# The second MLP's first product: seven block products a pair of ff chunks in place of eight, for two thirds of the tokens

## The chip, the cores and the metric

One Trainium2 chip, one core. The time is the device time of one launch in microseconds (us), the median of three runs. A profile of one more execution was taken by the hardware profiler; its times are from the start of its span.

## The reference

```python
# attention: q, k, v of 4 batches, 8 heads, 576 positions, 64 numbers a head;
# heads 0-3 look at the last 32 positions, heads 4-7 at every 4th of the last 128
x = attention(q, k, v)                            # (2304, 512) after the reshape
h = x @ moe_w_in;  r = np.maximum(h, 0.0)         # w_in (512, 2048)
x = (s * (r * r) + b) @ moe_w_out                 # w_out (2048, 512)
h = x @ moe2_w_in; g = h * np.cos(h)
return g @ moe2_w_out                             # (2304, 512)
```

## The kernel before

All numbers are fp32. A product in fp32 is made as three matmuls on parts cut in two (hi and lo, in the matmul's own fp32r format): hi·hi, hi·lo, lo·hi. Everything is kept transposed: features on the 128 partitions, tokens along the row. d_model = 512 is four chunks of 128, d_ff = 2048 is 16 ff chunks of 128.

**First MLP.** The tokens go through in five tiles `t` of 384, 384, 512, 512 and 512. A tile has 16 steps, one an ff chunk: `mm_in` makes h (PSUM, a ring of four banks from `bank`), `relu2` makes g and its two parts, and `mm_out` two steps later (LAG) adds to the four y banks. `relu2` takes ScalarE twice (Relu, then Square into r) and VectorE twice: a cast r → g hi (L496) and a subtraction r − g hi → g lo (L497). The attention of the next tile runs between the steps, in pairs of units ("duos", lists `DUO`): scores, softmax (`a_softmax`, `a_norm` on VectorE), transposition on TensorE (`a_transpose`, L350), and the product with v. `at((step, phase), f)` puts a piece of work behind a point of a step (phases 0, 1, 2). `y_out` scales a finished tile's y, and `y_park` sends it to DRAM (`y1`).

**The second MLP's weights** come as 64-bit words, and are prepared in the background of the first MLP by `w2_load`, `w2_float` (ScalarE), `w2_join` (VectorE) and `w2_cut`, at the steps listed in `BG_STEPS`. The 16 chunks of w_in, cut hi and lo, go to DRAM as `cut_in`. The 16 of w_out go to `whole_out`, and `job_load`, `job_sums` and `job_split` make from them the blocks that seven block products need (`cut_out`).

**Second MLP.** Three pieces of 768 tokens (i = 0, 1, 2). For each of the 48 (piece, ff chunk) pairs n, `mm_h` (L533) makes h in 24 matmuls of 128x384: four d_model chunks, three part products, two halves of 384 tokens. Then ScalarE and VectorE make h·cos(h) in four 128x768 operations: `cos_n` (ScalarE, the whole periods as int32), `cos_r` (VectorE, the rest), `cos_s` (ScalarE, Sin), `cos_g` (VectorE, times h). The product with w_out is made by seven block products where a plain one needs eight (Strassen's scheme in Winograd's form): 84 `unit`s of 12 matmuls of 128x384 (L642), `flush` forms sums of g, `unit_cut` cuts an operand hi (ScalarE cast, L587) and lo (VectorE subtraction, L588), `unit_load` brings 512 KB of `cut_out`. `evacuate`, `keep` and `send` empty PSUM and write the output through tile `o`, of which there are two. Units stand between the `mm_h`; those that are left run at the end, 26 of them.

All loads of weights (`wi` a chunk of `cut_in`, `wo` a unit's block), of x (`x_load`, 384 KB from `y1`) and the output's writes are issued by SyncE (SP), one after the other in program order: one that must wait for its buffer holds those behind it. `wi` and `wo` have four buffers each.

## Time and profile before

| what | before |
|---|---|
| time, median of 3 runs | 880.43 us (880.28 to 880.72) |
| the profiled execution | 880.15 us, of which 878.4 us are the span |
| TensorE (PE) busy | 870.6 us, 99%, 5148 matmuls |
| VectorE (DVE) busy | 594.2 us, 68% |
| ScalarE (ACT) busy | 477.1 us, 54% |
| the 16 DMA engines | 173.07 MB, mean 197 GB/s |

The span runs from the first to the last recorded event; the profiled time is longer by 1.75 us. A share is that engine's busy time over the span; PE's leaves 7.8 us of the span without a matmul. The first MLP runs to about 494 us; there the second MLP's h begins, and its 48 chunks and 84 units fill the rest.

### The profile page before, as it was taken

To read this page: it belongs to the slowest core of one execution; us is meant where nothing else is said; L and a number is where in the kernel's file an instruction comes from. 1 tells how busy PE (TensorE), PEld (TensorE's weight loads), DVE (VectorE), ACT (ScalarE), POOL (GpSimd) and SP (SyncE) were. 2 spreads that over 40 slices of the span, in tenths; PEclk is the share of its full clock that TensorE was granted. 3 is DMA by queue.
4 is the path that set the end of the run, shared out by engine and by line. 5 is a ranking of instruction groups with operands and counts; after the bars stand their busy time and mean duration, and the time that the engine had idled before them with its cause. 6 is when DMAs were issued, how large, how long until landed. Compare 5 with 4: busy or idle time off the path is not lost.

```text
span 878.4 us, 13747 instructions
## 1 busy us (share of the span) xinstructions
PE 870.6 (99%) x5148; PEld 778.9 (89%) x5148; DVE 594.2 (68%) x996; ACT 477.1 (54%) x1001; POOL 3.5 (0%) x10
## 2 busy tenths in 40 slices
...
PEclk9999999999999999999999999999999999999999
...
GB/s 251 337 231 252 95 93 148 96 103 157 151 127 125 111 200 165 167 135 148 262 321 386 344 359 121 140 218 188 183 226 214 203 185 172 206 220 146 219 268 209
DMA packets 76177, 173.07 MB, mean 197 GB/s; under 512 B 7152, under 2 KB 35280, under 8 KB 76112
## 3 DMA queue, kind: packets, MB, share of 16 engines
...
q8 instruction: 41, 0.67, 0.3%
...
## 4 chain that ended last, share of the span: by engine, by line
PE 94%; DVE 3%; ACT 1%; SPq 1%; DMA 1%; issue 0%; POOLq 0%; DVEq 0%
PE h L533 23%; PE yy_M L642 20%; PE h L424 6%; PE h L425 6%; PE h L426 6%; PE y L439 6%; PE y L441 6%; PE y L440 6%; PE y L436 4%; PE h L418 4%; PE sc L299 3%; PE pv L375 2%; PE tp L350 2%; DVE wa L148 1%; DVE wa L145 1%; DMA first_qk<-qk_d 1%
## 5 line engine op out<-in xcount | busy, mean ns | idle before, releaser
L533 PE MATMUL h<-x,wi 128*128 128x384 f32 x1152 | 205.1, 335 | 0.0
L533 PEld LDWEIGHTS h<-x,wi 128*128 128x128 f32 x1152 | 200.4, 188 | 0.2
L642 PE MATMUL yy_M<-op,wo 128*128 128x384 f32 x1008 | 180.2, 335 | 0.0
L642 PEld LDWEIGHTS yy_M<-op,wo 128*128 128x128 f32 x1008 | 175.7, 188 | 0.0
L542 ACT ACTIVATE i<-h 128x768 int32<-128x768 f32 x48 | 39.0, 813 | 149.1 <-PE h L533 149.1
L546 DVE SCALAR_TENSOR_TENSOR n<-i,h 128x768 f32<-128x768 int32 x48 | 45.8, 954 | 98.9 <-ACT i L542 98.9
L424 PE MATMUL h<-xs,wh 128*128 128x512 f32 (+1 forms) x256 | 98.7, 386 | 0.0
L439 PE MATMUL y<-g,wh 128*128 128x512 f32 (+1 forms) x256 | 97.7, 382 | 0.0
L426 PE MATMUL h<-xs,wl 128*128 128x512 f32 (+1 forms) x256 | 96.4, 376 | 0.0
L425 PE MATMUL h<-xs,wh 128*128 128x512 f32 (+1 forms) x256 | 96.3, 376 | 0.0
L441 PE MATMUL y<-g,wl 128*128 128x512 f32 (+1 forms) x256 | 96.2, 376 | 0.0
L440 PE MATMUL y<-g,wh 128*128 128x512 f32 (+1 forms) x256 | 96.1, 375 | 0.0
L588 DVE TENSOR_TENSOR op<-G,op 128x768 fp32r<-128x768 f32 x80 | 76.3, 955 | 19.0 <-ACT op L587 18.8
L587 ACT CAST op<-G 128x768 fp32r<-128x768 f32 x80 | 66.5, 833 | 36.2 <-PE yy_M L642 36.2
L329 ACT ACTIVATE sm<-sm,nmax 96x80 f32<-96x80 f32 (+1 forms) x140 | 49.5, 355 | 49.5 <-DVE nmax L326 49.5
L488 ACT ACTIVATE r<-h 128x512 f32<-128x512 f32 (+1 forms) x80 | 43.9, 549 | 48.5 <-PE h L426 40.9
L496 DVE CAST g<-r 128x512 fp32r<-128x512 f32 (+1 forms) x64 | 26.1, 408 | 55.9 <-ACT r L494 50.2
L560 DVE TENSOR_TENSOR G<-n,h 128x768 f32<-128x768 f32 x48 | 45.5, 949 | 15.9 <-ACT n L552 15.9
L424 PEld LDWEIGHTS h<-xs,wh 128*128 128x128 f32 x256 | 48.1, 188 | 7.8
L426 PEld LDWEIGHTS h<-xs,wl 128*128 128x128 f32 x256 | 48.1, 188 | 7.6
L441 PEld LDWEIGHTS y<-g,wl 128*128 128x128 f32 x256 | 48.0, 188 | 7.6
L425 PEld LDWEIGHTS h<-xs,wh 128*128 128x128 f32 x256 | 48.1, 188 | 7.3
...
## 6 DMA issues: line engine op xcount, KB each, us to landing
wo<-cut_out SPq DMA_DIRECT2D x84, 512.0 KB, 4.3
wi<-cut_in SPq DMA_DIRECT2D x48, 512.0 KB, 5.2
stage<-w SPq DMA_DIRECT2D x32, 512.0 KB, 7.6
raw<-w SPq DMA_DIRECT2D x32, 512.0 KB, 4.6
...
x<-y SPq DMA_DIRECT2D x12, 384.0 KB, 7.3
out_t<-o SPq DMA_DIRECT2D x11, 384.0 KB, 6.1
```

The costliest lines, as they stand in the source:

```text
L329: nc.scalar.activation(out=sm[:, j, :], in_=sm[:, j, :], func=AF.Exp, bias=nmax[:, j : j + 1], scale=1.0, accum_out=ssum[:, j : j + 1],)
L424: nc.tensor.matmul(h[:, : SIZES[t]], hi, x[:, 0, :], start=cc == 0, stop=False)
L425: nc.tensor.matmul(h[:, : SIZES[t]], hi, x[:, 1, :], start=False, stop=False)
L426: nc.tensor.matmul(h[:, : SIZES[t]], lo, x[:, 0, :], start=False, stop=cc == NCC - 1)
L439: nc.tensor.matmul(y[:, : SIZES[t]], hi, g[:, 0, :], start=fc == 0, stop=False)
L440: nc.tensor.matmul(y[:, : SIZES[t]], hi, g[:, 1, :], start=False, stop=False)
L441: nc.tensor.matmul(y[:, : SIZES[t]], lo, g[:, 0, :], start=False, stop=fc == NFC - 1)
L533: nc.tensor.matmul(h[:, t, :SB], wt, x[:, t * SB : (t + 1) * SB], start=cc == 0 and k == 0, stop=cc == NCC - 1 and k == 2,)
L546: nc.vector.scalar_tensor_tensor(out=ns[n], in0=ns.pop((n, "i")), scalar=-PERIOD, in1=hp[n], op0=ALU.mult, op1=ALU.add)
L587: nc.scalar.copy(x[:, 0], src)
L588: nc.vector.tensor_tensor(out=x[:, 1], in0=src, in1=x[:, 0].bitcast(F32), op=ALU.subtract)
L642: nc.tensor.matmul(b[:, eb, :SB], wt, g, start=fresh and k == 0 and z == 0 and n == 0, stop=k == 3 and z == 1 and n == 2, skip_group_check ...
```

## The change

For pieces i = 1 and 2, h is made by the same scheme as y: two ff chunks (a, b) by two halves of d_model, against the halves of d_model by two halves (384) of the tokens. A pair m = 0 to 15 takes seven products of 6 matmuls of 128x384 in place of eight. Four weights are loaded for a pair: A (chunk a), Y and X (sums of blocks of a and b) of 512 KB each, and Z (half of chunk b) of 256 KB. x comes as B11, B21, B22 and the sums T1 to T4. Bank `x` collects P1, P6, P5 and P3; `z` is copied from it after P1 (ScalarE) and then takes P2; copies u0 and u1 are taken after P6 and P5; bank `v` holds P7 and takes P4 last; `sums_b` (VectorE) adds v and u to chunk b's h in SBUF (`hs`).

Around it: w_in's sums (`s_sums`, `s_split`) are made in the first MLP after `CUTS`, which shifts `BG_STEPS`, the jobs and the transpositions; x's sums and their cuts (`x_sum`, `x_seven`) stand beside the first piece's h, chunks 5 to 12, those of piece 2 go through DRAM (`summed`) and come back in pair 7 (`x_late`); x is loaded from GpSimd's queue (POOL), 23 transfers, where SP issued 12; in tiles 2 to 4 g hi comes from a second Square on ScalarE, not from a VectorE cast; r has two buffers, not three; `o` has one, not two. Two units run before the pairs, three in each pair, one more in pairs 7 and 8, 32 at the end.

```diff
-BG = (0, 4, 9, 12, 7)
 BG_STEPS = (
-    (), (3, 6, 9, 14), (1, 3, 4, 6, 8, 9, 11, 13, 15), (0, 2, 3, 4, 5, 6, 7, 9, 10, 12, 13, 15), (0, 1, 2, 3, 4, 5, 6)
+    (), (3, 6, 9, 12, 14, 15), (0, 1, 2, 3, 4, 5, 6, 7, 8, 9, 10, 11, 13, 14), (2, 3, 5, 6, 8, 9, 11, 12, 14, 15), (2, 3)
 )
+CUTS = (
+    ((2, 11, 2), (2, 12, 2), (2, 13, 2)), ((2, 14, 2), (2, 15, 2), (3, 2, 0)), ((3, 3, 2), (3, 5, 0), (3, 6, 0)),
+    ((3, 6, 2), (3, 7, 1), (3, 8, 1)), ((3, 9, 2), (3, 10, 1), (3, 11, 1)), ((3, 12, 2), (3, 13, 1), (3, 14, 1)),
+    ((4, 0, 2), (4, 1, 2), (4, 3, 0)), ((4, 3, 2), (4, 4, 1), (4, 5, 2)),
+)
+JOBS_AT = 4, 6, 7, 8, 10, 11, 12, 13
+BG = tuple(len(steps) for steps in BG_STEPS)
+SQUARE_TWICE = 2
+NQ = NFC // 2
+PAIRS = 2 * NQ
+NN = 3
...
-        r = n % 2 if n < BG[1] else (n - BG[1]) % 3
-        place, tag = (late[0], f"raw{r}") if r < 2 else (wpool, "raw2")
+        r = raw_slot(n)
+        place, tag = (late[0], f"raw{r}") if r != 2 else (wpool, "raw2")
         raw_w["2", n] = place.tile([P, DM], I64, tag=tag, name=f"raw{n}")
...
-        hi = raw_w.pop(("2", n)).bitcast(F32R)[:, :DM]
...
+            raw_w.pop(("2", n))
...
+        hi = raw_w["2", n].bitcast(F32R)[:, :DM]
...
+    def s_sums(m):
...
+        x, y = s_pair(m)
+        for out_, p_, q_, op in (
+            (y[:, 1], b[:, 0], b[:, 1], ALU.add), (x[:, 0], y[:, 1], a[:, 0], ALU.subtract),
+            (x[:, 1], a[:, 0], b[:, 0], ALU.subtract), (y[:, 0], a[:, 1], x[:, 0], ALU.subtract),
+        ):
+            nc.vector.tensor_tensor(out=out_, in0=p_, in1=q_, op=op)
+    def s_split(m, h):
+        raw = raw_w["2", NFC + 2 * m + h]
+        x = raw.bitcast(F32)[:, DM:]
+        hi = raw.bitcast(F32R)[:, :DM]
+        nc.scalar.mul(hi, x, H_SCALE)
+        nc.vector.scalar_tensor_tensor(
+            out=x.bitcast(F32R), in0=x, scalar=H_SCALE, in1=hi.bitcast(F32), op0=ALU.mult, op1=ALU.subtract
+        )
+        nc.sync.dma_start(cut_s[m][:, h, 0], hi.bitcast(F32))
+        nc.sync.dma_start(cut_s[m][:, h, 1], x)
 
...
+        if t >= SQUARE_TWICE:
+            nc.scalar.activation(out=g[:, 0, :], in_=r, func=AF.Square)
         nc.scalar.activation(out=r, in_=r, func=AF.Square)
-        g = g_tile(t, fc)
-        nc.vector.tensor_copy(g[:, 0, :], r)
+        if t < SQUARE_TWICE:
+            nc.vector.tensor_copy(g[:, 0, :], r)
...
-        nc.sync.dma_start(lo.bitcast(F32), y1[i][:, cc, :])
+        nc.gpsimd.dma_start(lo.bitcast(F32), y1[i][:, cc, :])
...
+    def x_sum(i, name):
+        x = lambda n: xs7[i, n]
+        if name == "T3":
+            sub(x_full(i, "T3"), x("B22"), x("T1"))
+        elif name == "T1":
+            sub(x("T1"), x("T1"), x("B11"))
...
+        if i == 2:
+            nc.gpsimd.dma_start(x_from(i, name), x(name))
...
+    def x_late(i, name):
+        lo = x_tile(i, name, 1)
+        nc.gpsimd.dma_start(lo.bitcast(F32), x_from(i, name))
+        xs7[i, name] = lo.bitcast(F32)
+    def x_seven(i, name):
+        f = xs7.pop((i, name))
+        hi = x_tile(i, name, 0)
+        nc.scalar.copy(hi, f)
+        lo = x_tile(i, name, 1) if i == 1 else f.bitcast(F32R)
+        sub(lo, f, hi.bitcast(F32))
+        xo[i, name] = hi, lo
...
+    def w7_load():
...
+            src = cut_in[2 * (m % NQ) + 1][:, :, 256:]
+        else:
+            w7[m, what] = home[0].tile([P, 2, DM], F32R, tag=f"wi{ring7[0] % 4}", name=f"w{what}{m}")
+            ring7[0] += 1
+            k = m % NQ
+            src = cut_in[2 * k] if what == "A" else cut_s[k][:, "YX".index(what)]
+        nc.sync.dma_start(w7[m, what].bitcast(F32), src)
+    def product(m, name, b, fresh):
+        what, k = {"P1": "A0", "P2": "A1", "P5": "X1", "P6": "Y0", "P7": "Y1", "P3": "X0", "P4": "Z0"}[name]
+        w, k = w7[m, what], int(k)
+        part = lambda l, c: w[:, l, k * 256 + c * P : k * 256 + (c + 1) * P]
+        xh, xl = xo[1 + m // NQ, {"P1": "B11", "P2": "B21", "P3": "B22", "P4": "T4", "P5": "T1", "P6": "T2", "P7": "T3"}[name]]
+        for c in range(2):
+            for n, (wt, x) in enumerate(((part(0, c), xh), (part(0, c), xl), (part(1, c), xh))):
+                nc.tensor.matmul(
+                    b, wt, x[:, c], start=fresh and c == 0 and n == 0, stop=c == 1 and n == 2, skip_group_check=True
+                )
 
...
-        o = home[0].tile([P, 2, SB], F32, tag=f"o{sent[0] % 2}", name=f"o{i}_{quad}")
+        o = home[0].tile([P, 2, SB], F32, tag="o", name=f"o{i}_{quad}")
...
-                    at((p + 2, 0) if second and p + 1 < CUT + NFC else (p + 1, 2),
+                    at((p + 2, 1 if p + 2 in begin else 0),
...
+        steps_w2 = [t * NFC + step for t, steps in enumerate(BG_STEPS) for step in steps]
...
             at((p, 1), lambda k=k: w2_join(k))
-            at((p + 1, 0), lambda k=k: w2_cut(k))
+            if k < NFC:
+                at((p + 1, 0), lambda k=k: w2_cut(k))
+            elif k % 2:
+                m = (k - NFC) // 2
+                one, two, three = cut_steps(k)
+                at(one, lambda m=m: s_sums(m))
+                at(one, lambda k=k: w2_cut(k - 1))
+                at(two, lambda k=k: w2_cut(k))
+                at(three, lambda m=m: s_split(m, 0))
+                at(three, lambda m=m: s_split(m, 1))
...
-            p = NP - NFC + SUMS_FROM + (3 * i + 1) // 2
+            p = NP - NFC + JOBS_AT[i]
...
-        fresh_late = NP - NFC + BG_STEPS[-1][-1] + 2
+        fresh_late = NP - NFC + CUTS[-1][-1][1] + 1
...
             at((fresh_late, 2), lambda cc=cc: x_load(0, cc))
-            at((fresh_late + 1 + cc, 2), lambda cc=cc: x_cut(0, cc))
+            at((fresh_late + 3 + cc, 0), lambda cc=cc: x_cut(0, cc))
...
+        for n in range(1, NFC):
...
+            if n + 3 < NFC:
                 w_in_load(n + 3)
...
+                w7_load()
+            if 8 <= n < 12:
+                unit_load(n - 8)
+            if n == 2:
+                for name in RAW:
+                    x_raw(1, name)
+            if 5 <= n < 9:
+                x_raw(2, ("B12", "B22", "B11", "B21")[n - 5])
+            if n < NFC - 2:
...
+                x_sum(1 + (n > 8), ("T3", "T1", "T2", "T4")[(n - 5) % 4])
+            if n in (8, 9, 11):
+                x_seven(1, {8: "B11", 9: "T3", 11: "T2"}[n])
+            if n == 13:
+                cut_to(1)
+            if n == 14:
+                run_unit()
+                cut_to(nu + 2)
...
+        def sums_b(m, quad):
+            hs, v, u = b_side[m]
+            nc.vector.tensor_tensor(out=hs[:, quad], in0=v, in1=u[quad], op=ALU.add)
...
+        for m in range(PAIRS):
...
+            product(m, "P1", x, True)
+            used("P1")
+            if m:
+                cos_n(a - 1)
+            nc.scalar.copy(z, x)
+            if m:
+                cos_r(a - 2)
+                cos_r(a - 1)
+                cos_s(a - 2)
+                cos_s(a - 1)
+            run_unit()
+            evacuate()
+            if m == NQ:
+                x_seven(2, "B21")
+                x_seven(2, "T1")
+                cut_to(nu + 2)
+            if m:
+                cos_g(a - 2)
+                cos_g(a - 1)
+            else:
+                cos_s(a - 1)
+                cos_g(a - 1)
+            cut_to(nu + 2)
+            w7_load()
+            if m == 0:
+                x_seven(1, "B21")
+                x_seven(1, "T1")
+            product(m, "P7", v, True)
+            used("P7")
+            product(m, "P6", x, False)
...
+            w7_load()
+            nc.scalar.copy(u[0], x)
+            if m == 0:
+                x_seven(1, "B22")
+            if turn:
+                x_seven(2, "B11")
+            run_unit()
+            evacuate()
+            flush()
+            cut_to(nu + 2)
+            if m == NQ:
+                cut_to(nu + 3)
...
+            used("P2")
...
-                if n in x_at:
-                    x_cut(*x_at[n])
...
+            w7_load()
+            product(m, "P5", x, False)
...
+            nc.scalar.copy(u[1], x)
+            sums_b(m, 1)
+            if turn:
...
+            run_unit()
...
+            cut_to(nu + (3 if m == PAIRS - 1 else 2))
+            if m == NQ - 1:
+                run_unit()
+                evacuate()
+                flush()
+                cut_to(nu + 2)
+            product(m, "P3", x, False)
+            used("P3")
+            w7_load()
+            cos_n(a)
...
+            product(m, "P4", v, False)
+            sums_b(m, 0)
...
+        a = NFC + 2 * PAIRS
+        cos_n(a - 1)
+        cos_r(a - 2)
...
+        for k in range(2):
+            run_unit()
+            evacuate()
+            cut_to(nu + 3)
+            cos_s(a - 2 + k)
+            if k == 0:
+                cos_r(a - 1)
+            cos_g(a - 2 + k)
+            flush()
```

TensorE in a steady stretch of the second MLP, without row numbers. Before, chunk 31 of h behind two units (`yy0_M7`); `x1_0_0` and `x1_0_1` are hi and lo of d_model chunk 0 of piece 1:

```order
L642 MATMUL yy0_M7_6432<-op26_6604,wo26_6514 128x384 x12
L642 MATMUL yy0_M7_6432<-op27_6607,wo27_6528 128x384 x12
L533 MATMUL h2_31_6680<-x1_0_0_5208,wi31_6492 128x384 x2
L533 MATMUL h2_31_6680<-x1_0_1_5209,wi31_6492 128x384 x2
L533 MATMUL h2_31_6680<-x1_0_0_5208,wi31_6492 128x384 x2
L533 MATMUL h2_31_6680<-x1_1_0_5211,wi31_6492 128x384 x2
```

Now, pair 5, one row of each product (P1, a unit, P7, P6, a unit, P2, P5, a unit, P3, P4), the other rows of a product left out:

```order
L643 MATMUL zx5_6441<-xh1_B11_5494,wA5_6302 128x384
...
L770 MATMUL yy0_M2_6405<-op17_6386,wo17_6291 128x384 x12
L643 MATMUL v5_6442<-xh1_T3_5535,wY5_6351 128x384
...
L643 MATMUL zx5_6441<-xh1_T2_5613,wY5_6351 128x384
...
L770 MATMUL yy0_M2_6405<-op18_6421,wo18_6343 128x384 x12
L643 MATMUL zx5_6441<-xh1_B21_5832,wA5_6302 128x384
...
L643 MATMUL zx5_6441<-xh1_T1_5836,wX5_6365 128x384
...
L770 MATMUL yy0_M2_6405<-op19_6477,wo19_6380 128x384 x12
L643 MATMUL zx5_6441<-xh1_B22_5855,wX5_6365 128x384
...
L643 MATMUL v5_6442<-xh1_T4_5910,wz5_6395 128x384
```

Each product stands alone on one bank; two products at a time now stand between two units, where a chunk of 24 matmuls stood.

VectorE at the start of tile 2 of the first MLP (`sm`, `ssum`, `nmax` are the softmax of units 28 and 29, L340 to L342 their norm; `wa` is a w2 chunk). Before:

```order
L326 TENSOR_REDUCE nmax29_2328<-sm29_2326 128x3
L340 TENSOR_SCALAR ssum28_2322<-ssum28_2322 128x3
L341 RECIPROCAL rec28_2349<-ssum28_2322 128x3
L342 TENSOR_TENSOR sm28_2318<-sm28_2318,rec28_2349 128x288
L340 TENSOR_SCALAR ssum29_2330<-ssum29_2330 128x3
```

Now:

```order
L363 TENSOR_REDUCE nmax29_2359<-sm29_2357 128x3
L151 TENSOR_SCALAR wa2_6_2367<-wa2_6_2367 128x512
L154 TENSOR_SCALAR wa2_6_2367<-wa2_6_2367 128x512
L157 SCALAR_TENSOR_TENSOR wa2_6_2367<-raw6_2206,wa2_6_2367 128x512
L160 ISA wa2_6_2367<-raw6_2206,wa2_6_2367 128x1024
L377 TENSOR_SCALAR ssum28_2353<-ssum28_2353 128x3
L378 RECIPROCAL rec28_2389<-ssum28_2353 128x3
```

A w2 chunk's join now stands ahead of the norm and, behind that, of `y_out`.

SP's queue in the second MLP. Before:

```order
L510 DMA wi31_6492<-cut_in15_104 128x1024
L580 DMA wo26_6514<-cut_out_121 128x1024
L580 DMA wo27_6528<-cut_out_121 128x1024
L510 DMA wi32_6561<-cut_in0_89 128x1024
L673 DMA out_t<-o0_3_6563 128x2x384
L580 DMA wo28_6588<-cut_out_121 128x1024
```

Now, from the end of pair 5 to the end of pair 6:

```order
L634 DMA wA7_6558<-cut_in14_103 128x1024
L708 DMA wo24_6600<-cut_out_130 128x1024
L634 DMA wY7_6608<-cut_s7_129 128x1024
L634 DMA wX7_6622<-cut_s7_129 128x1024
L708 DMA wo25_6637<-cut_out_130 128x1024
L634 DMA wz7_6648<-cut_in15_104 128x2x256
L708 DMA wo26_6670<-cut_out_130 128x1024
L634 DMA wA8_6681<-cut_in0_89 128x1024
```

Four weights of h stand among three blocks of units for a pair, where two `wi` stood among four; wY7 takes the buffer that wA6 leaves.

## Rows read from the trace of the kernel before

**Rows 1.** The page: busy time of each engine, and the granted TensorE clock in 40 slices.
```profile
PE 870.6 (99%) x5148; PEld 778.9 (89%) x5148; DVE 594.2 (68%) x996; ACT 477.1 (54%) x1001; POOL 3.5 (0%) x10
PEclk9999999999999999999999999999999999999999
```
**Rows 2.** The chain of work that ended last, by engine.
```profile
PE 94%; DVE 3%; ACT 1%; SPq 1%; DMA 1%; issue 0%; POOLq 0%; DVEq 0%
```
**Rows 3.** Windows by stage; after the busy times: granted clock, DMA share, GB/s.
```profile
199.00:302.00 103.00, 103.00 (x678) 87.88 (x677) 58.67 (x130) 56.36 (x167) 0.00 (x0) 1.00 0.43 140
302.00:402.00 100.00, 99.63 (x581) 82.98 (x580) 66.52 (x134) 57.88 (x142) 0.00 (x0) 1.00 0.48 159
402.00:494.00 92.00, 92.00 (x408) 76.22 (x407) 74.98 (x130) 54.89 (x83) 0.00 (x0) 1.00 0.85 298
494.00:528.00 34.00, 34.00 (x191) 33.06 (x190) 15.98 (x18) 13.48 (x17) 0.00 (x0) 1.00 0.88 331
528.00:850.00 322.00, 322.00 (x1855) 322.00 (x1854) 203.96 (x225) 141.72 (x177) 0.00 (x0) 1.00 0.62 193
850.00:878.40 28.40, 24.47 (x142) 24.13 (x140) 12.29 (x14) 9.10 (x12) 0.00 (x0) 1.00 0.67 219
```
**Rows 4.** The chain from 470 to 530 us: start, duration, engine, line, count.
```profile
493.86 4.17 PE h L533 x24
...
503.46 24.96 PE h L533 x144
```
**Rows 5.** PE's waits: what it waited for, us in total, times, longest.
```profile
PE tp L350 <- DVE sm L342: 0.7, 2, 0.4
```
**Rows 6.** Groups by form, second MLP: busy us, mean ns of one, idle before.
```profile
L588 DVE TENSOR_TENSOR op<-G,op 128x768 fp32r<-128x768 f32 x80 | 76.3, 955 | 19.0 <-ACT op L587 18.8
L587 ACT CAST op<-G 128x768 fp32r<-128x768 f32 x80 | 66.5, 833 | 36.2 <-PE yy_M L642 36.2
L546 DVE SCALAR_TENSOR_TENSOR n<-i,h 128x768 f32<-128x768 int32 x48 | 45.8, 954 | 98.9 <-ACT i L542 98.9
L560 DVE TENSOR_TENSOR G<-n,h 128x768 f32<-128x768 f32 x48 | 45.5, 949 | 15.9 <-ACT n L552 15.9
L552 ACT ACTIVATE n<-n,quarter 128x768 f32<-128x768 f32 x48 | 44.6, 930 | 3.1 <-DVE n L546 3.1
L542 ACT ACTIVATE i<-h 128x768 int32<-128x768 f32 x48 | 39.0, 813 | 149.1 <-PE h L533 149.1
L664 ACT ACTIVATE o<-yy_M 128x384 f32<-128x384 f32 x1 | 0.5, 490 | 5.4 <-PE yy_M L642 5.4
```
**Rows 7.** Groups by form, first MLP and the half-width subtraction: the same columns.
```profile
L497 DVE TENSOR_TENSOR g<-r,g 128x512 fp32r<-128x512 f32 x48 | 33.2, 693 | 1.7
L494 ACT ACTIVATE r<-r 128x512 f32<-128x512 f32 x48 | 30.3, 632 | 1.5
L496 DVE CAST g<-r 128x512 fp32r<-128x512 f32 x48 | 20.4, 426 | 51.7 <-ACT r L494 46.1 <-PE sc L299 5.6
L219 DVE TENSOR_TENSOR job<-job 128x256 f32<-128x256 f32 x32 | 12.9, 422 | 4.0 <-DMA job<-whole_out 3.5
L201 DVE SCALAR_TENSOR_TENSOR wa<-wa,raw 128x512 fp32r<-128x512 f32 x16 | 11.0, 690 | 8.2 <-ACT raw L200 8.2
L139 DVE TENSOR_SCALAR wa<-wa 128x512 f32<-128x512 f32 x64 | 26.9, 421 | 3.9 <-ACT wa L134 3.9
L497 DVE TENSOR_TENSOR g<-r,g 128x384 fp32r<-128x384 f32 x16 | 8.9, 559 | 0.6
```
**Rows 8.** Loads of `wi`, from issue to landing.
```profile
DMA to landing us min/median/max: 3.1/5.2/9.9
```
**Rows 9.** Loads of `x`, from issue to landing.
```profile
DMA to landing us min/median/max: 4.3/7.3/10.8
```
**Rows 10.** DMA issues between 480 and 520 us: count, KB each, median us to landing.
```profile
wi<-cut_in SPq DMA_DIRECT2D x7, 512.0 KB, 8.1
```
**Rows 11.** DMA issues of the whole run, the output's writes.
```profile
out_t<-o SPq DMA_DIRECT2D x11, 384.0 KB, 6.1
```

More of the change, by code (lines that the diff above doesn't have):

```diff
@@ new lines, in x_tile @@
+    def x_tile(i, name, n):
+        tag = X_AT[SEVEN.index(name)][n]
+        place = home[0] if tag.startswith("xa") else late[0]
+        return place.tile([P, 2, SB], F32R, tag=tag, name=f"x{'hl'[n]}{i}_{name}")
+    def x_late(i, name):
[9 more added lines that the diff above has]
+        xo[i, name] = hi, lo
@@ new lines, in attention_then_two_mlps @@
+    loads7 = [(m, what) for m in range(PAIRS) for what in "AYXZ"]
+    ring7 = [0]
+    w7 = {}
+    def w7_load():
+        if not loads7:
+            return
+        m, what = loads7.pop(0)
+        if what == "Z":
+            w7[m, what] = home[0].tile([P, 2, 256], F32R, tag="wz", name=f"wz{m}")
+            src = cut_in[2 * (m % NQ) + 1][:, :, 256:]
+        else:
+            w7[m, what] = home[0].tile([P, 2, DM], F32R, tag=f"wi{ring7[0] % 4}", name=f"w{what}{m}")
[3 more added lines that the diff above has]
+        nc.sync.dma_start(w7[m, what].bitcast(F32), src)
@@ L910, in attention_then_two_mlps @@
         ps_o = ctx.enter_context(tc.tile_pool(name="ps_o", bufs=1, space=PSUM, reuse_waits="tile", side="right"))
-        mm_h(2, ps_o, "p2")
+        third = ExitStack()
+        wide = [third.enter_context(tc.tile_pool(name="ps_w", bufs=1, space=PSUM, reuse_waits="tile", side="right"))]
+        mm_h(2, wide[0], "p2")
         mm_h(3, ps_o, "yy")
@@ L933, in cut_to, with run_unit @@
                 cutn[0] += 1
+        def run_unit():
+            nonlocal nu
+            cut_to(nu + 1)
+            unit(nu)
+            nu += 1
         cos_n(0)
         cos_r(0)
-        for n in range(1, NH):
+        for n in range(1, NFC):
             if n >= 4:
-                mm_h(n, *((ps_h, "p0"), (ps_h, "p1"), (ps_o, "p2"))[(n - 4) % 3])
-            if n >= 1 and n + 3 < NH:
+                mm_h(n, *((ps_h, "p0"), (ps_h, "p1"), (wide[0], "p2"))[(n - 4) % 3 if n < NFC - 1 else 0])
+            if n + 3 < NFC:
@@ L965, in attention_then_two_mlps @@
-            for _ in range(at_unit.get(n, 0)):
-                cut_to(nu + 1)
-                unit(nu)
-                nu += 1
-            ahead = at_unit.get(n + 1, 0)
-            cut_to(nu + ahead + (at_unit.get(n + 2, 0) if ahead < 2 else max(0, n + 3 - NH)))
-        cos_s(NH - 1)
-        cos_g(NH - 1)
+            if 5 <= n < 13:
+                x_sum(1 + (n > 8), ("T3", "T1", "T2", "T4")[(n - 5) % 4])
+            if n in (8, 9, 11):
+                x_seven(1, {8: "B11", 9: "T3", 11: "T2"}[n])
```

129 lines of the change are left out of this document (93 added, 36 removed).

## Prediction

> **What bounds the kernel now.** I read the page's totals first: PE is busy 870.6 of 878.4 us, and the granted clock is 9 tenths or more in every slice [rows 1]; in the windows by stage it is 1.00, the upper of the two levels, 2.4 GHz [rows 3]. Then the chain of waits: 94% of it is PE's own work [rows 2]. Then the windows by stage: from 528 to 850 us PE has no gap at all, while VectorE is busy 203.96 of 322 us (63%), ScalarE 44%, the DMA engines 62% at 193 GB/s [rows 3]. So in the second MLP the time is a number of matmuls times the pace of one, as long as nothing makes PE wait. The pace is in the chain: 24 matmuls of h in 4.17 us, then 144 in 24.96 us [rows 4], 29.13 / 168 = 173.4 ns for a 128x384 one. The units run at that pace too: the window 528 to 850 mixes both, 1855 recorded in 322 us, 173.6 ns [rows 3]. I call P = 6 matmuls = 1.04 us a product, U = 12 = 2.08 us a unit, 24 = 4.16 us a plain chunk; a pair with its three units takes 78 matmuls, 13.52 us.
>
> **What the change takes away.** Matmuls of h before: 48 chunks x 24 = 1152. After: 16 x 24 for piece 0, and 16 pairs x 42 = 672, 1056 in all. That is 96 fewer, 96 x 0.1734 = **16.65 us**. The units stay 84, and the first MLP keeps its matmuls. The copies and sums that pay for it run on engines that are not full, so the question is where PE has to wait for them.
>
> **Inside a steady pair** (t from the start of P1, in PE's order P1 U1 P7 P6 U2 P2 P5 U3 P3 P4). ScalarE's copy of a 128x384 bank costs about 490 ns (the one such eviction in the trace, [rows 6]), VectorE's 128x384 addition 559 ns [rows 7].
> - P6 adds to bank x from t = 4.16 and must wait for the copy z: P1 ends at 1.04, `cos_n` may stand ahead (813 ns, [rows 6]), then 490: done at 2.4. Spare 1.8 us.
> - P5 starts at 8.32 and waits for u0; P6 ends at 5.20, copy done at 5.7 to 5.9. Spare 2.4.
> - P3 starts at 11.44 and waits for u1; P5 ends at 9.36, done at 9.9. Spare 1.5.
> - P4 starts at 12.48 in bank v and waits for `sums_b(1)`, 0.56 behind u1: 10.5, or 11.4 if one 955 ns subtraction [rows 6] is ahead. Spare 1 to 2.
> The load of the two engines allows it. ScalarE: two `cos_n`, two `cos_s`, three casts, three copies: 2 x 0.813 + 2 x 0.930 + 3 x 0.833 + 3 x 0.49 = 7.5 of 13.5 us. VectorE had 0.633 x 16.65 = 10.5 us for two chunks with four units; now one subtraction (0.955) less and two `sums_b` (1.12) more, 10.7 of 13.5, 79%. I cost a steady pair at 0. If the cover is gone, each pair pays (rival 1).
>
> **Pairs with more work.** In pair 0 five more cuts of x (a cast of about 0.83 and a subtraction of about 0.95, [rows 6]) share VectorE with U2's operand, and P4 wants T4 about when its cut ends, 12.6 us; pair 8 has four cuts and an extra unit. Walked through with these durations, they leave 0 to 0.2 and 0.3 to 0.6 us of wait. I take **+0.6** for both, bounds 0 and 3 (one cut, both engines, late in each: 2 x 1.8 is 3.6, less the spare).
>
> **SP's queue.** Weights Y of pair m+1 go in the buffer of A of pair m, so the load is issued when P2 of pair m ends, and P7 of pair m+1 needs it 48 matmuls later (P5, U3, P3, P4, P1, U1): 8.32 us. X and a unit's block are behind it in the queue and are needed later. A 512 KB load lands after 3.1 / 5.2 / 9.9 us (min, median, max over the run, [rows 8]), and after 8.1 (median) in the densest stretch [rows 10], where the share is 0.85 to 0.88 at 298 to 331 GB/s [rows 3]. The pairs ask for 6.5 blocks of 0.524 MB in 13.52 us, 252 GB/s, against 6 in 16.65 us before, 189 (193 measured). By 0.62 x 252 / 189 the share is about 0.83. An estimate between the two stretches: 5 to 7.5 us, so most loads land in time and a few do not. I take **+0.4** for the few; bounds 0 and 15 x (9.9 - 8.32) = 24.
>
> **x by POOL's queue.** The trace shows no load issued there; the nearest row is SP's x: 4.3 / 7.3 / 10.8 us [rows 9]. Piece 1's blocks are issued at chunk 2 and first used at chunk 5, three chunks or 12.5 us later; piece 0's at step 6 of the last tile for a cut at step 9: 2.3 steps of 24 matmuls of 92.00 / 408 = 225.5 ns [rows 3] are 12.4 us. Piece 2's, in pair 7, have till pair 8: about 8.5 us for the first. Taken at 7.3: 0; at 10.8: 2.3 for the first and some 0.7 behind it. And SP's queue loses 12 transfers. A rule speaks against this step. The row: VectorE's cast of 128x512 takes 426 ns, its two-input subtraction of the same width 693 [rows 7]; neither says anything of a DMA. The Trainium skill, page "SBUF — State Buffer", box on the "DVE blocks DMA" trap, says that a DMA from GpSimd's queue has its descriptors written by GpSimd's cores, which a VectorE operation in a two-port mode, such as an fp32 copy, locks out. No run here shows it. In the second MLP of the changed kernel VectorE has two-input operations only, so by that rule the sum stays the same; if the lock held for these as well, each load would start later by up to one operation, 0.96 us, and only the load in pair 7 would tell: about +1.
>
> **Beside the first h** (chunks 5 to 12). A chunk has 4.16 us. VectorE has `cos_r`, `cos_g` (0.954 + 0.949) and one or two of sum and subtraction (0.95 each), at most 4.8 us in a chunk that has three; three h banks in PSUM stand between. I take 0.
>
> **First MLP.** ScalarE gets 48 Squares (L494, 632 ns) and 16 cuts of sums (the same width, 633): 30.3 + 10.1 = 40.4 us over tiles 2 to 4; there (199 to 494) it is busy 56.36 + 57.88 + 54.89 = 169 of 295 us, then 71%. VectorE loses 48 casts (20.4 us) and gets 32 sums of 128x256 (422, 13.5) and 16 subtractions (690, 11.0): +4 on 200 [rows 3, 7]. Neither fills. What can hurt is order: at the start of tile 2 a w2 chunk's join (two operations of 421 and two longer ones of 690 and about twice that, 2.9 us) now stands ahead of the norm and of `y_out`, and TensorE waits for `y_out` before the new tile's first product into the same banks. The transpositions are a step later, 5.4 us, which covers the norm; `y_out` has a slack of about what the join takes. A similar place is in tile 3. I take **+0.7**; bounds 0 and 4 (one whole join, and one operation). The later transpositions also remove the wait for `sm`, the longest 0.4 [rows 5], which is the 0.37 us by which PE falls short in 302 to 402 [rows 3]: **-0.37**. The other one (0.3) I leave.
>
> **The tail.** 32 units are left and not 26, all at PE's pace. With one `o`, a write must have landed before the next `send`; the last products' sends are four units apart, 8.3 us, and a write takes 6.1 [rows 11]: 0.
>
> **Sum.** 880.15 (profiled) - 16.65 - 0.37 + 0.7 + 0.6 + 0.4 = 864.83; the median of the runs stands 0.28 above the profiled execution: **865.1 us**. What two measurements of this kernel can tell apart is about 0.2%, 1.8 us.
>
> **Rivals.**
> 1. *A wait in every pair.* VectorE at 79% takes operations in program order, and one that comes late holds the next; if half a microsecond is lost in each of 16 pairs, 865.1 + 8 = 873. For it: nine links between three engines in 13.5 us. Against: the least spare is 1 us. Chance 0.08.
> 2. *The other side: Y late on SP.* If Y's landing is typically beyond 8.32 us, each of 15 pairs pays the excess; from 8.32 + 16.65 / 15 = 9.4 us the change is slower, and at 10 us it is 865 + 25 = 890. For it: 9.9 has been seen, and the share goes up. Against: the densest stretch had a median of 8.1. Chance 0.06, half of it slower than before.
> 3. *x late by POOL.* Loads at 10.8 us or more, at pair 8 and at piece 0: +2 to 6, 867 to 871. For it: x had the slowest landings of SP. Against: 12 us of lead nearly everywhere. Chance 0.06.
> 4. *The matmuls don't get cheaper by their number.* Every product works on one bank with a wait possible at either end. If a matmul of these 672 took 198 ns and not 173.4, the 16.65 are gone: about 880. Against: units do just this at 173.6. Chance 0.03, spread over no change and slower.
> The forecast itself, 863.2 (no waits at all) to 868.5, has 0.77.
>
> **Range and chances.** 863.2 to 870.0 holds the forecast and most of rival 3, a little over 8 in 10; rivals 1, 2 and 4 lie above. Faster 0.94, within 0.2% 0.02, slower 0.04.
>
> **What would show it.** Right: 5052 matmuls, h's part 1056; PE's share still 99%; no line of PE's waits above 1 us except small ones at pairs 0 and 8; wY landing at 5 to 8 us. Wrong: PE waiting for `z`, `u`, `v` or `op` sixteen times, or for DMA `w`; a wait at the first step of tiles 2 or 3 of over 2 us; ScalarE late with g in tiles 2 to 4. The likeliest mistake is a wait at the links between SP, VectorE and PE, which the trace of before cannot show, since there PE never waits in this stage.

## The result, and the profile after

The changed kernel takes 871.99 us in the median (870.44 to 872.86, 4 runs) against 880.36 on the same chip: ratio 0.9903, 95% interval 0.9886 to 0.992. It is faster, by 8.4 us and not by 15. The forecast was 865.1 and the range ended at 870.0: both too low. The profiled execution is the fastest of the four, 870.44 us with a span of 868.7.

The page after: the engines' totals and the chain of work that ended last, which answer to [rows 1] and [rows 2].

```profile
PE 858.0 (99%) x5052; PEld 763.1 (88%) x5052; DVE 621.4 (72%) x1042; ACT 536.7 (62%) x1119; POOL 18.1 (2%) x33
...
PE 68%; issue 17%; DMA 6%; DVE 4%; ACT 3%; SPq 1%; POOL 0%; DVEq 0%; POOLq 0%
```

5148 - 5052 = 96 matmuls are gone, as counted. "issue 17%" in the chain is no new bound: from 523 to 671 us the chain runs back along POOL's queue (its longest piece is 108.34 us between two transfers, from 562.80 on), and in that stretch PE has no gap. Windows by stage after. Before, PE was busy 84.00 us of the first, and 103.00, 99.63 and 92.00 of the next three [rows 3].

```profile
115.00:199.00 84.00, 82.16 (x595) 77.14 (x595) 64.32 (x133) 56.40 (x162) 0.00 (x0) 1.00 0.39 126
199.00:302.00 103.00, 102.07 (x672) 86.89 (x669) 69.56 (x151) 73.43 (x198) 0.00 (x0) 1.00 0.55 181
302.00:402.00 100.00, 100.00 (x639) 83.66 (x638) 66.10 (x137) 69.51 (x167) 0.00 (x0) 1.00 0.56 192
402.00:494.00 92.00, 92.00 (x407) 76.20 (x406) 61.81 (x102) 58.47 (x90) 2.31 (x4) 1.00 0.79 269
...
528.00:560.00 32.00, 32.00 (x186) 32.00 (x186) 24.09 (x27) 15.25 (x19) 1.66 (x3) 1.00 0.69 235
560.00:840.00 280.00, 279.68 (x1602) 278.38 (x1601) 210.25 (x248) 152.89 (x215) 4.93 (x8) 1.00 0.77 263
```

PE's new gaps are early: 1.84 us between 115 and 199, 0.93 between 199 and 302, where it had none. From 560 to 840, nearly all of the pairs, it idles 0.32 us. The granted clock is at its upper level in all of these windows. The list of PE's waits after says who held it (what it waited for, us in total, times, longest); of before, [rows 5] answers to the third row: one of its two waits, at 343.6 us, is gone, and one at 196.2 is new.

```profile
PE h L461 <- DVE sm L354: 1.7, 6, 0.5
...
PE tp L387 <- DVE ssum L377: 0.8, 1, 0.8
...
PE tp L387 <- DVE sm L379: 0.7, 2, 0.4
PE y L477 <- DVE g L537: 0.3, 1, 0.3
PE zx L643 <- ACT u L1175: 0.2, 1, 0.2
```

To see what these cost I set the first product of each step of the first MLP beside that of before. Tile 1 begins 0.11 us earlier than before; the first product of the second MLP's h comes at 497.63 against 493.70, 3.93 later. The delay grows by 0.5 to 0.7 at each of the six waits for `sm`, 3.3 us in all, and once by 1.5 at the wait for `ssum`; it falls by 0.7 where before waited at 343.6. For the six the list has 1.7 us, about half. It counts from the end of the last matmul, but without a stop the next one begins before that end. Before, behind the same transposition without a wait:

```profile
193.03 0.82 PE L350 MATMUL tp<-ident,sm 96*80 96x96 f32 x8
193.63 0.42 PE L439 MATMUL y<-g,wh 128*128 128x384 f32 x1
```

The next product begins 0.60 us after the transposition here, and 1.08 after it in the stop below, whose gap is 0.25: 0.48 us lost by the gap and the overlap. The longer first matmul explains little of it, 0.45 us against 0.42 here.

One of the six, PE's instructions and then VectorE's (start us, duration, instruction, idle before it and who ended that):

```profile
183.83 1.18 PE L336 MATMUL sc<-qk 128*96 128x80 f32 x12
...
186.98 0.82 PE L387 MATMUL tp<-ident,sm 96*80 96x96 f32 x8
188.06 0.45 PE L461 MATMUL h<-xs,wh 128*128 128x384 f32 x1 [0.25 <-DVE sm L354]
```

```profile
187.52 0.49 DVE L354 SCALAR_TENSOR_TENSOR sm<-sc,m_d 96x320 f32<-96x320 f32 x1 [1.78 <-PE tp L387]
...
192.01 0.43 DVE L151 TENSOR_SCALAR wa<-wa 128x512 f32<-128x512 f32 x1 [2.58 <-ACT wa L146]
...
194.37 0.16 DVE L377 TENSOR_SCALAR ssum<-ssum 96x4 f32<-96x4 f32 x1
```

The scores of a new duo end at 185.0. VectorE's first operation on them stands still 1.78 us, until the old duo's transposition, now behind the scores in PE's order, has read the softmax's buffer. PE's next h takes, in the ring of four banks, the bank that these scores are in, and waits for that operation. Behind it comes the second loss: a w2 chunk's join waits 2.58 us for ScalarE, with the norm behind it in VectorE's queue, and the transposition at 195.41 waits for the norm.

The pairs, by the first matmul of P1 in pairs 6 to 9:

```profile
656.09 0.34 PE L643 MATMUL zx<-xh_B,wA 128*128 128x384 f32 x1
...
669.69 0.34 PE L643 MATMUL zx<-xh_B,wA 128*128 128x384 f32 x1
...
685.75 0.34 PE L643 MATMUL zx<-xh_B,wA 128*128 128x384 f32 x1
...
702.26 0.34 PE L643 MATMUL zx<-xh_B,wA 128*128 128x384 f32 x1
```

A steady pair takes 13.60 us (13.52 forecast), and all thirteen (0 to 6, 9 to 14) are within 0.03 of it. Pair 7, with 90 matmuls, takes 16.06 and pair 8 16.51, where 90 at 173.4 ns are 15.61. Pair 8 takes 16.48 to 16.51 in every profile whose code is the same there; pair 7 varies, from 15.68 to 16.37.

### The profile page after: what moved, and what is told of

Same layout as the page of the kernel before. It is cut to its first block, busy times and chain, and to the rows that moved or that the text cites. A ratio compares the mean times of both kernels' runs of the same rounds, so it can differ in the third digit from the quotient of the medians.

```text
span 868.7 us, 13870 instructions
## 1 busy us (share of the span) xinstructions
PE 858.0 (99%) x5052; PEld 763.1 (88%) x5052; DVE 621.4 (72%) x1042; ACT 536.7 (62%) x1119; POOL 18.1 (2%) x33
## 4 chain that ended last, share of the span: by engine, by line
PE 68%; issue 17%; DMA 6%; DVE 4%; ACT 3%; SPq 1%; POOL 0%; DVEq 0%; POOLq 0%
PE yy_M L770 13%; PE h L461 6%; PE h L463 6%; PE h L462 6%; PE y L476 6%; PE y L477 6%; PE y L478 6%; PE zx L643 5%; PE y L473 4%; PE h L455 3%; PE sc L336 2%; PE pv L412 2%; PE v L643 2%; DMA stage<-w 2%; PE tp L387 1%
## 5 line engine op out<-in xcount | busy, mean ns | idle before, releaser
L770 PE MATMUL yy_M<-op,wo 128*128 128x384 f32 x1008 | 184.2, 335 | 0.1
L537 DVE TENSOR_TENSOR g<-r,g 128x512 fp32r<-128x512 f32 (+1 forms) x64 | 42.0, 656 | 47.1 <-ACT r L534 45.1
L662 PE MATMUL h<-x,wi 128*128 128x384 f32 x384 | 67.1, 336 | 0.0
L662 PEld LDWEIGHTS h<-x,wi 128*128 128x128 f32 x384 | 66.7, 188 | 0.2
L477 PEld LDWEIGHTS y<-g,wh 128*128 128x128 f32 x256 | 48.2, 188 | 7.8 <-DVE g L537 0.7
L476 PEld LDWEIGHTS y<-g,wh 128*128 128x128 f32 x256 | 48.1, 188 | 6.9
L473 PE MATMUL y<-g,wa 128*128 128x385 f32 x128 | 44.2, 488 | 0.0
```

The lines of the kernel that those rows point to most:

```text
L473: nc.tensor.matmul(y[:, : SIZES[t] + 1], w[:, es], g, start=fc == 0, stop=fc == NFC - 1)
L476: nc.tensor.matmul(y[:, : SIZES[t]], hi, g[:, 0, :], start=fc == 0, stop=False)
L477: nc.tensor.matmul(y[:, : SIZES[t]], hi, g[:, 1, :], start=False, stop=False)
L662: nc.tensor.matmul(h[:, t, :SB], wt, x[:, t * SB : (t + 1) * SB], start=cc == 0 and k == 0, stop=cc == NCC - 1 and k == 2,)
L770: nc.tensor.matmul(b[:, eb, :SB], wt, g, start=fresh and k == 0 and z == 0 and n == 0, stop=k == 3 and z == 1 and n == 2, skip_group_check ...
```

## The experiments

The edits are to the changed kernel if nothing else is said. Its own ratio to before was 0.9903 in the first four runs, 0.9914 in a second set. "First h" is the start of the second MLP's h: 493.70 us before, 497.63 after; small offsets at the start of tile 1 (-0.1 to +0.3) are taken off where I give a loss, so the change's is 4.04.

**The transpositions back at their old points (e1_tp).**

```diff
-                    at((p + 2, 1 if p + 2 in begin else 0),
+                    at((p + 2, 0) if second and p + 1 < CUT + NFC else (p + 1, 2),
```

> The changed kernel with the transpositions of the attention back at the points of before; nothing else. In the profile after, the second MLP's h begins 3.9 us later than before, where I had forecast 0.3. Theory A (the later transposition, 6 places): scores' PSUM banks and the softmax's buffer are held until the transposition, so the next h of the first MLP waits; then the six waits of h for VectorE's sm (1.7 us in all, 2.8 with what each costs around it) go away, h of the second MLP begins 2.5 to 3 us earlier, and the time falls by as much, to about 869. Theory B (VectorE's norm is late because of the added joins and sums, and the later point only hides it): the six waits turn into waits of the transposition for the norm, and the time stays within 1 us of 872.

Measured: 883.19 us, ratio to before 1.0029 (1.0018 to 1.0041); the first h at 509.77, a loss of 15.9. Both theories were half right. In tile 1, up to the step at 191 us, the delay is 0.0 where the change has 1.5: theory A there. In tiles 2 and 3 the transpositions run into the norm, as theory B says, and at a price that neither had. PE's waits, and one of them on VectorE:

```profile
PE tp L387 <- DVE ssum L377: 6.1, 7, 2.1
PE tp L387 <- DVE sm L379: 2.8, 9, 0.4
PE tp L387 <- ACT raw L147: 2.1, 1, 2.1
```

```profile
227.96 0.43 DVE L151 TENSOR_SCALAR wa<-wa 128x512 f32<-128x512 f32 x1 [2.02 <-ACT wa L146]
...
230.32 0.16 DVE L377 TENSOR_SCALAR ssum<-ssum 128x3 f32<-128x3 f32 x1
```

The waits are 11.0 us of the 15.9. A part of the rest is the clock. Windows around the stops that end at 215.9, 380.2 and 403.0 us (PE busy, granted clock, DMA share, GB/s):

```profile
214.00:216.00 2.00, 0.54 (x4) 1.00 0.06 23
218.00:220.00 2.00, 2.00 (x6) 0.50 0.52 199
382.00:384.00 2.00, 2.00 (x7) 0.50 0.32 124
402.00:404.00 2.00, 0.72 (x7) 1.00 0.52 196
```

Behind the first two stops, of 1.46 and 2.10 us, the granted clock is at the lower level for some 15 matmuls in all; a 128x512 one lasts 0.63 us there and not 0.39, and begins 0.43 us behind the one before and not 0.23. 15 x 0.2 makes 3 us, an estimate. Behind the third, of 2.09 us, it doesn't fall. All twelve runs of this kernel have a mean clock of 0.993 to 0.998, where the runs of the changed kernel have 0.999 or 1.

So the later transposition pays for the denser background work: without it the gain would be lost. It costs some 2 to 3 us itself.

**The same move alone, in the kernel before (e6_before_tp)**: the diff above the other way round.

> The kernel before with the transpositions moved a step later, nothing else. Theory A: the six waits of h for sm appear here too, without any of the change's added work; the second MLP's h begins 2 to 3 us later (less 0.4 for the removed wait at 343.6 us), time 882 to 883. Theory B (they need the added VectorE work): within 0.5 us of 880.4, no wait of h for sm.

Measured: 882.46, ratio 1.0025 (1.0015 to 1.0035), first h at 496.39, a loss of 2.65, and six waits:

```profile
PE h L424 <- DVE sm L317: 1.8, 6, 0.6
```

Theory A: they need none of the change's added work. The 2.65 is what is left of 3.4 at the six waits, since the wait at 343.6 is gone here too.

**A third buffer for the softmax (e7_sm).**

```diff
+    sm_ = att.enter_context(tc.tile_pool(name="att_s", bufs=1))
-        sm = d["sm"] if "sm" in d else ap_.tile([nr, nb, nk], F32, tag="sm", name=f"sm{i}")
+        sm = d["sm"] if "sm" in d else sm_.tile([nr, nb, nk], F32, tag=f"sm{i % 3}", name=f"sm{i}")
```

> The changed kernel with three buffers for the softmax's sm in place of two, the transpositions left late. Theory A1 (the hold is the sm buffer: the first softmax of a new duo may not write before the old duo's transposition has read): with a third buffer the first scores' bank comes free early, the six waits of h go, 2 to 2.8 us won, about 869.5. Theory A2 (the hold is only the position of the transposition's banks in the ring of four): no change, 872, six waits still there.

Measured: 868.86, ratio 0.9872 (0.9859 to 0.9886), first h at 495.70; of the loss of 4.04, 1.85 is gone. Five of six waits vanish. The first softmax operation now starts right behind the scores, and only the second waits for the transposition:

```profile
184.92 0.48 DVE L355 SCALAR_TENSOR_TENSOR sm<-sc,m_d 96x320 f32<-96x320 f32 x1
...
186.78 0.49 DVE L355 SCALAR_TENSOR_TENSOR sm<-sc,m_d 96x320 f32<-96x320 f32 x1 [0.86 <-PE tp L388]
```

It is A1, the buffer: h needs only the first scores' bank. Two things stay. The sixth wait, at 289.80 (0.47 us), is not the buffer's: there the softmax stands, without a gap, behind a join, four sums, a cut and a g on VectorE. And the softmax's exponentials are still late, since on ScalarE they stand behind the copy of the old duo's transposition; the wait for `ssum` stays too (1.0 us).

```profile
186.78 0.85 ACT L392 COPY pt<-tp 80x384 f32<-80x384 f32 x2 [2.76 <-PE tp L388]
187.52 0.37 ACT L367 ACTIVATE sm<-sm,nmax 96x80 f32<-96x80 f32 x1
```

**The join one step earlier in tile 1 (e2_join).**

```diff
-    (), (3, 6, 9, 12, 14, 15), (0, 1, 2, 3, 4, 5, 6, 7, 8, 9, 10, 11, 13, 14), (2, 3, 5, 6, 8, 9, 11, 12, 14, 15), (2, 3)
+    (), (3, 6, 9, 11, 14, 15), (0, 1, 2, 3, 4, 5, 6, 7, 8, 9, 10, 11, 13, 14), (2, 3, 5, 6, 8, 9, 11, 12, 14, 15), (2, 3)
```

> The changed kernel with one w2 chunk's join in tile 1 at step 11 in place of 12. Theory A': at step 14 the transposition waits (0.8 + 0.3 us) only since this join of four operations stands ahead of the norm on VectorE; then both waits go, 1.0 to 1.5 us are won, about 870.7. Rival: the norm is late because the softmax began 2 us late (held by the transposition before it): the waits stay, 0 to 0.3 us won.

Measured: 868.68, ratio 0.9867 (0.9853 to 0.9881). The wait for `ssum` is gone and the loss is 2.80, 1.24 less, as theory A' said. The time fell by more than that; the profiled execution, at 870.78, was the slowest of the four, and its waits of y for g were 1.3 us and not 0.3. So something varies from run to run; that is the next experiment. The rival, a norm late by the late softmax, is right in part. In e1_tp the softmax is not held, but the norm stands behind the same join, and the delay grows by 0.8 at this place, where it grows by 1.5 after the change: the join alone costs 0.8, the late softmax the rest. VectorE in e1_tp:

```profile
185.69 0.48 DVE L354 SCALAR_TENSOR_TENSOR sm<-sc,m_d 96x320 f32<-96x320 f32 x1
...
190.17 0.43 DVE L151 TENSOR_SCALAR wa<-wa 128x512 f32<-128x512 f32 x1 [2.57 <-ACT wa L146]
...
192.53 0.16 DVE L377 TENSOR_SCALAR ssum<-ssum 96x4 f32<-96x4 f32 x1
```

**The changed kernel again, and the last job a step later (after_again, e9_jobs).** Between 494 and 510 us VectorE stands still for a load of `whole_out`. After, and in e9_jobs (the job's row of each):

```profile
498.26 1.68 DVE L256 TENSOR_TENSOR job<-job 128x256 f32<-128x256 f32 x4 [4.54 <-DMA job<-whole_out]
499.86 0.68 DVE L537 TENSOR_TENSOR g<-r,g 128x512 fp32r<-128x512 f32 x1
...
504.47 0.69 DVE L537 TENSOR_TENSOR g<-r,g 128x512 fp32r<-128x512 f32 x1 [1.43 <-PE y L477]
```

```profile
498.50 1.68 DVE L256 TENSOR_TENSOR job<-job 128x256 f32<-128x256 f32 x4 [0.16 <-DMA job<-whole_out]
```

```diff
-JOBS_AT = 4, 6, 7, 8, 10, 11, 12, 13
+JOBS_AT = 4, 6, 7, 8, 10, 11, 12, 14
```

> The changed kernel itself once more, so that the runs beside it are compared on one chip, and to see what differs from one execution to the next (870.4 to 872.9 us in the first four). If theory J holds (next run), the time from the second MLP's first h to the first pair's P1 differs between executions (76.9 us in the first profile, 78.2 and 78.4 in two kernels with the same code there), and nothing else does. 870 to 873 us.

> The changed kernel with the last job of w_out's sums back at step 14 of the last tile (13 in the change). Theory J: its load is issued a step before it is used, lands 9 to 11 us after its issue in the densest stretch, VectorE stands still for it (4.5 to 6.3 us), the g of the last two chunks is behind it and y waits for g; a step later the load is there: waits of y for g go from 0.3 to 1.3 us down to 0.2 or less, the first P1 comes 76.3 us after the first h, 0.6 to 2 us are won, and the runs lie closer together. Rival: the job's cut now stands in front of the last chunk's g and the wait only moves by a chunk: within 0.5 us of the changed kernel.

Measured: the changed kernel 872.9 (870.02 to 875.28, 6 runs), e9_jobs 870.73 (870.46 to 870.83, 4 runs), ratios 0.9914 (0.9898 to 0.993) and 0.9894 (0.9881 to 0.9907). In e9_jobs no y waits for g, and the first P1 comes 76.24 us after the first h; in the changed kernel 76.89 and 77.32. Theory J held for the waits. Eight profiles have the job at step 13. In seven of them its sums begin, when the load has landed, 0.4 to 2.2 us behind the first h, and the way from the first h to the first P1 is longer than 76.24 by just that, within 0.03 us; in the eighth (e5_cast) they begin 1.3 us ahead of it, and the way is 76.24. In the time the two intervals overlap: a gain is not shown. The runs lie 0.4 us apart and not 5.3, but those of e11_three, with the same edit, spread over 2.3.

The job is not all that varies. The two profiles of the changed kernel lie 2.1 us apart: 0.6 arise before the first h, 0.4 are the job's, 0.1 pair 7's, and 1.0 arise in the tail, where in the second a unit waits 0.7 us for its `wo` and in the first none does. That tail wait has no experiment of its own.

**The loads of x by SP (e3_sp)**: in `x_load`, `x_raw`, `x_sum`, `x_late` `nc.gpsimd.dma_start` becomes `nc.sync.dma_start`.

> The changed kernel with all 23 transfers of x issued by SP as before, none by POOL. If POOL's queue is what costs (the load of B11 in pair 7 lands 8 us after P1, and a unit waits 0.4 us), 0.4 to 2 us are won, and the spread of the runs shrinks. If the queue doesn't matter, within 0.5 us. If the loads of x, which wait for their buffers, hold up the weights behind them in SP's order, pairs 7 and 8 wait for wY or wX and it is slower by 1 to 6 us.

Measured: 871.82, ratio 0.9912 (0.99 to 0.9925): no difference to the changed kernel. But the parts moved: pairs 0 to 6 are the same 13.60, pair 7 takes 15.68 and pair 8 19.28 us, 2.8 more than with POOL:

```profile
687.24 2.20 PE L770 MATMUL yy_M<-op,wo 128*128 128x384 f32 x11 [0.68 <-DVE op L716]
690.99 0.44 PE L643 MATMUL zx<-xh_T,wY 128*128 128x384 f32 x1 [0.50 <-ACT zx L1147]
692.47 2.38 PE L770 MATMUL yy_M<-op,wo 128*128 128x384 f32 x12 [0.17 <-DVE o L800]
695.25 0.44 PE L643 MATMUL zx<-xh_B,wA 128*128 128x384 f32 x1 [0.40 <-ACT u L1175]
```

The waits are for VectorE and ScalarE, not for weights as I had thought. It is the weights that hold up x: on SP two loads of `xl_T` stand behind a wY that waits for its buffer, and are issued 8.9 and 9.4 us after the start of pair 7; on POOL they were issued 4.5 and 5.6 us after it. From issue to landing they took no longer (6.5 and 6.9 us; 7.1 on POOL). ScalarE, in order, then stands 4.8 us for the first of them, with the copies behind it. SP's queue and ScalarE here, and POOL's first load of `xl_T` in the changed kernel:

```profile
677.63 0.32 SPq L634 DMA_DIRECT2D wY<-cut_s  x1
678.00 0.90 SPq L607 DMA_DIRECT2D xl_T<-summed  x2
684.49 0.84 ACT L613 CAST xh_T<-xl_T 128x768 fp32r<-128x768 f32 x1 [4.83 <-DMA xl_T<-summed]
```

```profile
674.18 0.57 POOL L607 DMA_DIRECT2D xl_T<-summed  x1 [2.31 <-PE v L643]
```

POOL's queue costs nothing that this shows.

**Four edits together (e10_best)**: those of e7_sm, e2_join and e9_jobs, and in pair 8

```diff
             if m == NQ:
                 x_seven(2, "B21")
-                x_seven(2, "T1")
...
             nc.scalar.copy(u[0], x)
+            if m == NQ:
+                x_seven(2, "T1")
```

> The changed kernel with four edits: a third sm buffer, the join of tile 1 at step 11, the last job at step 14, and in pair 8 the cut of x's T1 behind the copy u0. If the losses that were found add up (2.7 + 1.2 + 0.6 to 1.9 + 0.5 to 0.9), the second MLP's h begins at 494.3 us (before: 493.7), pairs 7 and 8 take 16.0 and 15.8 us, and the time is 865.5 to 867. If some of them share one cause, it stays at 868 to 869.

Measured: 867.48, ratio 0.9857 (0.9844 to 0.987). The first h comes at 494.33: what the two edits win in the first MLP adds up, a loss of 0.4 is left. The edit in pair 8 was wrong: 16.80 us, with a wait of 0.6 for T1's lo part. **Without it (e11_three):**

> The last combination without its edit in pair 8: third sm buffer, join of tile 1 at step 11, last job at step 14. The edit in pair 8 made PE wait 0.6 us for T1's lo part there; without it pair 8 takes 16.5 us and not 16.8: 867.2, 0.3 less than 867.5; h of the second MLP still begins at 494.3 us.

Measured: 866.96 (866.48 to 868.75), ratio 0.9852 (0.9837 to 0.9867), pair 8 at 16.48; the first h at 495.08 and not at 494.3, a loss of 1.45, with one wait of 0.7 for `sm` that e10_best did not have, though the two kernels are the same up to there. A load of w2 landed later: ScalarE waits for it, the join on VectorE waits for ScalarE, and the softmax stands behind the join.

```profile
182.29 0.67 ACT L146 ACTIVATE wa<-raw 128x512 f32<-128x512 f32 x1 [1.18 <-DMA raw<-w]
```

The two intervals overlap; this is the lowest median I have.

**The transpositions ahead of the scores (e12_tp0)**, with the edits of e2_join and e9_jobs:

```diff
-                    at((p + 2, 1 if p + 2 in begin else 0),
+                    at((p + 2, 0),
```

> The changed kernel with all late transpositions at phase 0 of their step, so that where a new duo starts they stand ahead of its scores and not behind; two sm buffers as in the change; join at step 11 and last job at step 14 as in the run beside it. If the loss of the first MLP is the order scores, transposition, h (the scores' bank is the one that h takes next, and its reader waits for the transposition), all six waits of h for sm go without a third buffer: h of the second MLP begins at 493.7 to 494.3, 866.5 to 867.5. If the norm is late at that point, two microseconds earlier in the step, the transpositions wait for it instead: 868 to 871.

Measured: 871.63, ratio 0.9901 (0.9884 to 0.9917), first h at 500.30. The time of the second case, but by a third mechanism. The waits for `sm` are gone and the norm is in time; now the second scores take the bank of the h just made, and wait for ScalarE's Relu to read it:

```profile
PE sc L336 <- ACT r L525: 5.6, 6, 1.5
```

With four banks, either order has somebody waiting for the bank of a neighbour; the third buffer is what shortens it.

**g hi by VectorE's cast (e5_cast).**

```diff
-SQUARE_TWICE = 2
+SQUARE_TWICE = 5
```

> The changed kernel with g hi in tiles 2 to 4 by VectorE's cast, as before, in place of ScalarE's second Square; nothing else. By the sum (VectorE has room for 20.4 us over 295) the first MLP's time is the same within 1 us and the two are equal. Rival: VectorE, which also carries the joins, the sums and the softmax in order, is where tiles 2 and 3 are tight; then the transpositions and h wait for it more than now (3.9 us in all), 2 to 8 us slower.

Measured: 870.96, ratio 0.9893 (0.9878 to 0.9908): not told from the changed kernel. The first MLP loses 1.5 us more (first h at 499.08; the waits of h for `sm` grow from 1.7 to 3.1), but no y waits for g at the turn to the second MLP, and the first P1 comes 76.24 us after the first h, 0.65 less. Of the 1.5 about 0.5 arise in tile 1, where the two kernels are alike, 1.0 in tile 2. So VectorE is a little tight in tile 2. Of the turn it says nothing: the first h came later and the job's load 0.45 us earlier, so that the job was done in time.

**No extra unit in pair 8 (e13_unit8)**: the block `if m == NQ: run_unit(); evacuate(); flush()` behind P2 and its `cut_to` are left out.

> The changed kernel without the extra unit in pair 8 (33 units in the tail). Pair 8 takes 16.5 us there against 15.7 for its 90 matmuls. If the excess is the copy u0, late behind two casts of x on ScalarE (0.4 us before P2), and a unit's operand behind the rest (0.4 us), the pair takes 14.0 us for 78 matmuls: 0.4 left of 0.9, the time 0.4 lower. If the extra unit was what gave the cuts of x their time, P5 or P3 wait for T1 or B22 and the excess grows by 0.5 to 2.

Measured: 873.13, ratio 0.9917 (0.9903 to 0.9932). Pair 8 takes 15.55 us for 78 matmuls, an excess of 1.95 over a steady pair; with the unit it was 0.8 at the same pace. Its time is not told from the changed kernel's, as the intervals overlap. The second case: the wait for the copy u0 stays at 0.2, and P3 waits for x:

```profile
694.35 0.44 PE L643 MATMUL zx<-xh_B,wA 128*128 128x384 f32 x1 [0.24 <-ACT u L1175]
700.17 0.44 PE L643 MATMUL zx<-xl_B,wX 128*128 128x384 f32 x1 [1.17 <-DVE xl_B L696]
```

## Why the prediction was wrong

The profiled execution stands 5.6 us above the 864.83 of the sum: 3.6 in the first MLP, 1.1 by the pace, 0.65 by a job, 0.75 in pairs 7 and 8, less the 0.4 taken for late loads, which makes 5.7.

- **The main term was right.** 96 matmuls are gone, and a pair takes 13.60 us. The pace of 173.4 ns was slightly low: 13.60 / 78 = 174.4 ns. Over the 14 pairs without an extra unit that is 1.1 us. Before, the matmuls of h began 173.6 ns apart in this stage and those of the units 173.9, so a third of it was there to be read.
- **"First MLP", +0.7 and -0.37, is the step that failed: it measured +3.9.** I wrote that the transpositions are a step later "which covers the norm", and costed the move at less than nothing. The wait that it removes was rightly seen, and gave 0.7 (it is the shorter one of [rows 5]; the longest, 0.38 us at 48.3, is there after as before). But I had not asked what the transposition holds in the meantime: the softmax's buffer, and by that the scores' bank that the next h takes. e6_before_tp gives it 2.65 us with no other change; e7_sm shows that the buffer is the link. The join ahead of the norm I had seen, but at the wrong place (tiles 2 and 3, `y_out`) and with slack; it cost 1.2 at the end of tile 1 (e2_join), of which 0.8 without a late softmax (e1_tp). The two edits together win 3.6 of the 4.04 in e10_best, and 2.6 in e11_three, where a load came late.
- **A job moved by a step was not costed at all.** Its load has one step, not two, in the stretch where the landing of a `wi` took 8.1 us in the median before [rows 10]. It cost 0.65 us in the first profile and 1.1 in the second. The medians of e9_jobs and the changed kernel on one chip lie 2.2 apart, but their intervals overlap, and in the second profile a wait in the tail cost as much as the job. Why the median of the first four runs lies 1.5 above the profiled execution is open: the job is one cause of the spread, and not the only one.
- **Pairs 0 and 8, +0.6: 0 and 0.9 measured,** and 0.45 in pair 7, which the sum had at nothing (0.1 in the profiles where it takes 15.68). In pair 8 the copy u0 came late behind two casts of x and one of a unit on ScalarE, and P2 waited for it, 0.5 us of the 0.9. My list of four did not have this link: z and x are halves of one tile, and z's product waits for the copy of x.
- **Steady pairs at 0 and Y on SP's queue: right**, and the +0.4 for loads was not needed. In all of these kernels a steady pair took 13.60. wY, from issue to landing, after (against 8.32 us of lead, and my estimate of 5 to 7.5, which was too high; [rows 8] answers to it):

```profile
DMA to landing us min/median/max: 3.2/4.1/7.1
```

- **Rival 3, x by POOL: no.** Its loads landed in 4.6 to 8.0 us in pair 7, and e3_sp is not faster. No run here puts a VectorE copy beside these loads. In e5_cast two casts of 0.43 us stand beside the loads of piece 0, which landed in 5.6 to 7.1 us, against 4.8 to 7.8 without the casts; a hold as short as that can't be told from the spread, so the rule quoted with it is not tested.
- **Rival 1** had the right kind of cause, an operation that waits in order on VectorE, but in the first MLP, where I had counted occupancy: 70% said nothing of who stands behind whom.
